# Output matmuls of a gated linear attention: four 32-column tiles in place of two 64-column tiles

## The chip, the cores and the metric

The kernel runs on one core of one Trainium2 chip. The metric is the device time of that core in microseconds (us). Eleven runs of the kernel before in one session took 195.06 to 195.69 us, 0.3% apart. Each timed execution also has a span (first to last instruction of the program, about 2 us shorter than the time) and a mean granted clock of TensorE. A run that is over 1.5% above the fastest of the same kernel counts as slow and is left out of every ratio here. A median here is over all runs, slow ones too.

Names in the profile: PE is TensorE's matmul, PEld its weight load, DVE is VectorE, ACT is ScalarE, POOL is GpSimd, SP is SyncE, which issues most of the transfers ("SPq" is its queue). L303 is line 303 of that kernel's source.

## The reference

A gated linear attention (4 batches, 8 heads, 768 steps, head size 48) feeds a matmul, a gate h·cos(h), and a second matmul (3072 tokens, 384 → 2048 → 384).

```python
for t in range(S):
    state = alpha[:, :, t, :, None] * state + einsum('bhd,bhe->bhde', k[:, :, t], v[:, :, t])
    y[:, :, t] = einsum('bhd,bhde->bhe', q[:, :, t], state)
# x: y as [3072 tokens, 384]
h = x @ w_in
out = (h * cos(h)) @ w_out
```

## The kernel before

The sequence is cut into 24 chunks of 128 steps (6 per batch). The kernel is a list of units in a hand-made order, one string for all engines; the letter names the unit, the number the chunk (or pair of chunks).

```python
ORDER = """
k1 a0 a3 a1 k0 v1 q0 a2 q2 i0 x12 c0 v3 d0 k2 M0 i1 x7 c1 k3 K0 d1 q1 K1 q3 P1 O0 x13 T0 v0 l1 t0
... (cut)
m9 E6 S9 D10 P11 Q4 u9 b9 D11 V24 z4 R12 V25 u10 v13 H18 K12 v14 b10 H16 D12 h18 H19 q15 g18 h16 o5
... (cut)
"""
```

Units that matter here: `a k q v` load one chunk of alpha, keys, queries and values; `K R` scale keys and queries on POOL; `D` transposes them by DMA; `A` and `m` make and mask the scores; `S u b` compute the state; **`Y` (one chunk) and `Q` (two chunks) are the output matmuls**, `z` copies their result out of PSUM; `H h g` are the first matmuls, the activation and the gate; `V e o` are the second matmuls, their copy and the store; `x` is a fixed number of warm-up matmuls.

The output of a chunk, transposed, is 384 rows (8 heads x 48) by 128 steps, kept as three groups of 128 PSUM partitions. Each row gets two contributions: U, from the state of earlier chunks (one matmul for a pair of heads, absent in the first chunk of a batch), and V, from the scores inside the chunk (one matmul per head). The kernel before splits the 128 partitions into two column tiles of 64:

```python
    def outputs(j, t):
        ...                                   # vs: values, padded; U: state; qT, A: moving operands
        mms = []
        for n in range(2 * 3):                # six tiles of 64 rows
            g, tt = n // 3, n % 3
            a = []
            if j % NC != 0:
                for p, c0 in (((0, 0),), ((0, 64), (1, 96)), ((1, 160),))[tt]:
                    c0 += 2 * C * g
                    a.append((U[:, c0 : c0 + 64], qT[...]))
            for r in range(2):
                ...
                a.append((vs[:, c0 : c0 + 64], A[...]))
            mms.append(a)
        streams = [...]                       # tiles 0, 2, 4 to partitions 0-63; 1, 3, 5 to 64-127
        for i in range(max(map(len, streams))):
            for half, stream in enumerate(streams):
                if i < len(stream):
                    kt, start, stop, lhsT, rhs = stream[i]
                    nc.tensor.matmul(t[64 * half : 64 * half + 64, kt * C : (kt + 1) * C],
                                     lhsT, rhs, start=start, stop=stop, skip_group_check=True)
```

The boundaries of 64 rows cut across heads of 48, so a tile needs 2 V and 1 or 2 U matmuls: 12 V + 8 U = 20 in a chunk, 10 in each stream. A weight load goes with every matmul (448 of each in the trace).

## Time and profile before

| | before |
|---|---|
| median time | 195.58 us (195.28 to 195.73, 4 runs) |
| PE busy, share of the span | 95% |
| output matmuls | 448, in 13 bursts (Y0, Y1, Q1 to Q11) |
| one burst of 40 (Q), first to last start | 1.088 us |

The page of the kernel before, its busy times (us, share of the span, instructions) and its chain of waits (the chain of work that ended last, by engine and by line):

```profile
PE 182.5 (95%) x1990; PEld 131.8 (68%) x1994; DVE 117.7 (61%) x138; ACT 120.1 (62%) x133; POOL 81.6 (42%) x128
...
PE 66%; DMA 13%; SPq 6%; ACT 4%; issue 4%; DVE 3%; POOL 2%; ACTq 0%; DVEq 0%
PE one L362 31%; PE two L341 21%; DMA w<-in_moe_w_out_dram 10%; PE two L303 6%; SPq L158 5%; PE two L243 3%; DVE g_sb L352 3%; DMA v_sb<-in_v_dram 2%; ACT c_sb L347 2%; PE two L191 2%; SPq L161 2%; ACT L347 1%; PE one L257 1%; POOL w L167 1%; PE two L193 1%
```

A busy PE alone would not prove a bound, since ends of matmuls are modelled; the chain shows that from 43 us on the time mostly follows PE. Four stretches of it (59 to 64, 85 to 88, 111 to 117 and 127 to 131 us) pass mainly through ACT and DVE, most of it the gate, and PE waits at their ends for 0.13, 1.0, 0.83 and 0.05 us. L303, the output matmuls, holds 6% of the chain. The same chain in order of time (start us, length us, what), its output bursts Q4 and Q7 alone:

```profile
80.61 1.24 PE two L303 x40
...
123.96 1.24 PE two L303 x40
```

The windows of the second half (window, its length, busy us and instructions per engine, granted clock, DMA share, GB/s):

```profile
124.00:164.00 40.00, 39.95 (x455) 29.68 (x455) 27.76 (x28) 33.92 (x35) 19.80 (x30) 1.00 0.87 162
```

PE has 0.05 us to spare in 40; the other engines have 6 us or more. By these numbers a microsecond less of PE work here should be a microsecond less of time, as long as the others keep up; that is an estimate.

The groups of L303 (out<-in, tile, moving shape, count | busy us, mean ns | idle before):

```profile
L303 PE MATMUL two<-A_sb,vpb 128*64 128x128 bf16 x264 | 13.2, 220 | 0.1
L303 PE MATMUL two<-qkT,ub 128*64 128x128 bf16 x152 | 11.8, 222 | 0.7 <-POOL ub L262 0.7
...
L303 PEld LDWEIGHTS <-vpb 128*64 128x64 bf16 x288 | 12.8, 110 | 0.5 <-issue 0.3
```

The 220 ns is the length of one matmul's record; the starts in one tile lie only 56 ns apart, so the cost is read from the starts. Of burst Q7, ns from its first start, read from the trace:

```
before:  0 4 | 80 83 | 137 140 | 192 195 | 247 251 | ...   pairs, 56 ns apart
```

Two tiles start mostly 3 to 4 ns apart and both take their next matmul 56 ns later: a row of two costs 56 ns. The first step alone is 80 ns.

### The profile page before, as it was taken

The numbers are of one execution on the slowest core, as the hardware profiler recorded it, in microseconds if no ns is written. First come the engines' busy times: TensorE is split into PE (matmuls) and PEld (weight loads), VectorE is DVE, ScalarE is ACT, GpSimd is POOL, SyncE is SP. The second block draws the span as 40 slices with busy tenths as digits, with TensorE's granted clock in tenths as the row PEclk, the third lists the DMA queues.
The fourth block names the chain that finished last, engine by engine and source line by source line (L and its number), as shares of the span: only waits on it lengthen the run. The fifth ranks groups of instructions, "written<-read, shape, count | busy, mean of one in ns | idle before, by whom it ended". The sixth has DMA issues, their size and how long they took to land.

```text
span 192.9 us, 4781 instructions
## 1 busy us (share of the span) xinstructions
PE 182.5 (95%) x1990; PEld 131.8 (68%) x1994; DVE 117.7 (61%) x138; ACT 120.1 (62%) x133; POOL 81.6 (42%) x128
## 2 busy tenths in 40 slices
PE   7997889989999999997999998999999999999993
PEld 2444468957688687685777685786786786876861
DVE  5025784844847928829828438748758578596450
ACT  2540344744768668947739567789999982361632
POOL 3317950055294655571190656271239761030000
PEclk9999999999999999999999999999999999999999
DMA  6999999999989999999989999999998762200112
GB/s 127 188 187 188 146 190 188 184 196 194 190 192 176 205 233 207 188 168 196 268 162 192 175 214 218 175 227 205 149 217 158 135 152 34 85 0 3 41 41 82
DMA packets 123092, 31.23 MB, mean 162 GB/s; under 512 B 117184, under 2 KB 122304, under 8 KB 123072
## 3 DMA queue, kind: packets, MB, share of 16 engines
q1 hardware_dynamic: 120192, 27.80, 85.0%
q0 software_dynamic: 2880, 3.15, 10.1%
q8 instruction: 15, 0.25, 0.5%
q14 instruction: 5, 0.04, 0.1%
HBM read 25.17 MB, written 4.72 MB: 155 GB/s over the span
## 4 chain that ended last, share of the span: by engine, by line
PE 66%; DMA 13%; SPq 6%; ACT 4%; issue 4%; DVE 3%; POOL 2%; ACTq 0%; DVEq 0%
PE one L362 31%; PE two L341 21%; DMA w<-in_moe_w_out_dram 10%; PE two L303 6%; SPq L158 5%; PE two L243 3%; DVE g_sb L352 3%; DMA v_sb<-in_v_dram 2%; ACT c_sb L347 2%; PE two L191 2%; SPq L161 2%; ACT L347 1%; PE one L257 1%; POOL w L167 1%; PE two L193 1%
## 5 line engine op out<-in xcount | busy, mean ns | idle before, releaser
L352 DVE TENSOR_TENSOR g_sb<-two,c_sb 128x1024 bf16<-128x1024 f32 x48 | 58.0, 1221 | 27.7 <-ACT c_sb L347 27.2
L362 PE MATMUL one<-w,g_sb 128*128 128x384 bf16 x384 | 69.5, 327 | 1.4 <-DVE g_sb L352 0.8
L341 PE MATMUL two<-xT,w 128*128 128x256 bf16 (+1 forms) x624 | 68.4, 264 | 1.0 <-DVE g_sb L352 1.0
L347 ACT ACTIVATE c_sb<-two,halfpi 128x1024 bf16<-128x1024 f32 x48 | 52.6, 1113 | 19.5 <-PE two L341 19.0
L341 PEld LDWEIGHTS <-w 128*128 128x128 bf16 x624 | 56.7, 98 | 9.7 <-issue 1.1
L362 PEld LDWEIGHTS <-g_sb 128*128 128x128 bf16 x384 | 35.3, 98 | 24.0 <-DVE g_sb L352 1.7
L206 POOL TENSOR_TENSOR kqb<-k_sb,icp 128x384 bf16<-128x384 f32 x24 | 23.9, 997 | 20.5 <-DMA k_sb<-in_k_dram 12.6
L262 POOL TENSOR_TENSOR ub<-sc,Em 128x384 bf16<-128x384 f32 x20 | 16.6, 829 | 33.1 <-DVE sc L272 31.8
L248 DVE TENSOR_TENSOR A_sb<-two,mask_f 128x1024 bf16<-128x1024 f32 x24 | 28.5, 1217 | 2.6 <-PE two L243 2.6
L212 POOL TENSOR_TENSOR kqb<-q_sb,cp 128x384 bf16<-128x384 f32 x22 | 21.9, 998 | 9.4 <-DMA q_sb<-in_q_dram 5.7
L366 ACT ACTIVATE o_sb<-one 128x384 f32<-128x384 f32 x24 | 11.7, 492 | 15.5 <-PE one L362 15.5
L347 ACT ACT_TABLE_LOAD x11 | 14.1, 1283 | 9.9 <-PE two L341 6.2
L216 POOL CAST vpb<-v_sb 128x384 bf16<-128x384 f32 x24 | 12.0, 504 | 17.2 <-DMA v_sb<-in_v_dram 9.3
L375 PE MATMUL one<-warm 128*128 128x512 bf16 x62 | 17.1, 418 | 2.2 <-DVE warm L102 1.2
L185 ACT ACTIVATE lnab<-a_sb 128x768 bf16<-128x768 f32 (+1 forms) x13 | 10.3, 794 | 12.5 <-DMA a_sb<-in_alpha_dram 12.4
L201 ACT ACTIVATE icp<-two 128x768 f32<-128x768 f32 (+1 forms) x13 | 9.9, 761 | 11.8 <-PE two L193 9.0
L272 DVE TENSOR_TENSOR sc<-one,ub 128x384 f32<-128x384 f32 x20 | 11.0, 552 | 8.2 <-PE one L257 7.9
L321 DVE CAST xT<-two 128x768 bf16<-128x768 f32 x11 | 10.5, 958 | 8.4 <-PE two L303 8.4
L179 ACT ACT_TABLE_LOAD x11 | 14.1, 1283 | 0.9 <-PEq L404 0.7
L303 PE MATMUL two<-A_sb,vpb 128*64 128x128 bf16 x264 | 13.2, 220 | 0.1
L303 PEld LDWEIGHTS <-vpb 128*64 128x64 bf16 x288 | 12.8, 110 | 0.5 <-issue 0.3
L375 PEld LDWEIGHTS <-warm 128*128 128x128 bf16 x66 | 6.4, 104 | 9.6 <-issue 3.6
(42 smaller groups left out, 114.1 us busy)
## 6 DMA issues: line engine op xcount, KB each, us to landing
k_sb<-in_k_dram SPq DMA_DIRECT2D x24, 192.0 KB, 4.6
a_sb<-in_alpha_dram SPq DMA_DIRECT2D x24, 192.0 KB, 4.3
v_sb<-in_v_dram SPq DMA_DIRECT2D x24, 192.0 KB, 4.4
q_sb<-in_q_dram SPq DMA_DIRECT2D x24, 192.0 KB, 4.2
out_dram<-o_sb SPq DMA_DIRECT2D x24, 192.0 KB, 3.7
w<-in_moe_w_in_dram POOLq DMA_DIRECT2D x2, 768.0 KB, 10.0
w<-in_moe_w_out_dram POOLq DMA_DIRECT2D x2, 768.0 KB, 17.7
qkT<-kqb SPq DMA_TRANSPOSE x16, 3.8
```

The costliest lines, as they stand in the source:

```text
L179: nc.scalar.preload_act_table_set("natural_log_exp_and_others")
L206: nc.gpsimd.tensor_tensor(out=kqb[j % 4][:, 0, :, 0:D], in0=k_t[j % 6], in1=icp_t[j // 2 % 3][:, j % 2].rearrange("s (h d) -> s h d", h=H) ...
L212: eng.tensor_tensor(out=kqb[j % 4][:, 1, :, 0:D], in0=q_t[j % 6], in1=cp.rearrange("s (h d) -> s h d", h=H), op=ALU.mult)
L216: nc.gpsimd.tensor_copy(out=vpb[j % 4][:, :, 0:D], in_=v_t[j % 6])
L248: nc.vector.tensor_tensor(out=A_t[j % 4].rearrange("s (h t) -> s h t", h=H), in0=two[("A", j)].rearrange("s (h t) -> s h t", h=H), in1=mas ...
L262: eng.tensor_tensor(out=ub[j % 3][:, :, 0:96].rearrange("r p (a e) -> r p a e", a=2), in0=src.rearrange("r p (a e) -> r p a e", a=2), in1= ...
L303: nc.tensor.matmul(t[64 * half : 64 * half + 64, kt * C : (kt + 1) * C], lhsT, rhs, start=start, stop=stop, skip_group_check=True)
L341: nc.tensor.matmul(t[:, m * n : (m + 1) * n], w1[:, kk, f * C : (f + 1) * C], x_t[g % 3][:, kk, bs].rearrange("r b t -> r (b t)"), start=( ...
L347: nc.scalar.activation(out=c_s.take((name, i)), in_=two[(name, i)], func=AF.Sin, bias=halfpi, scale=1.0)
L352: nc.vector.tensor_tensor(out=g_t[g % 3][:, fs, bs], in0=shaped(two[(name, i)], name), in1=shaped(c_s[(name, i)], name), op=ALU.mult)
L362: nc.tensor.matmul(one[("o", j)][:, 0:DM], g_t[j // 2 % 3][:, f, j % 2], w2[:, f], start=(f == 0), stop=(f == NF - 1))
L375: nc.tensor.matmul((one.free or two.free)[0][:, 0:512], warm[:, 0:C], warm, start=True, stop=True)
```

## The change

Cut the 128 partitions into four column tiles of 32 rows. With 32-row groups a pair of heads (96 rows) is exactly three groups: rows 0-31 of the first head, its rows 32-47 with rows 0-15 of the second, rows 16-47 of the second. Each group needs one U and 1, 2 or 1 V: 12 U + 16 V = 28 matmuls a chunk, more than before, but in four streams of 7 in place of two of 10. Over the kernel 448 matmuls become 624.

```diff
-        for n in range(2 * 3):
-            g, tt = n // 3, n % 3
-            ... (cut)
+        def group(g):
+            p, r = g // 3, g % 3
+            mms = []
             if j % NC != 0:
+                mms.append((U[:, p * C + 32 * r : p * C + 32 * r + 32],
+                            qT[:, (NP + p) * C : (NP + p + 1) * C]))
+            for h, off in (((0, 0),), ((0, 32), (1, -16)), ((1, 16),))[r]:
+                h += 2 * p
+                mms.append((vs[:, h * VS + off : h * VS + off + 32],
+                            A[:, ACOL[h] * C : (ACOL[h] + 1) * C]))
+            return [(g // 4, i == 0, i == len(mms) - 1) + m for i, m in enumerate(mms)]
+
+        streams = [sum((group(g) for g in range(c, 12, 4)), []) for c in range(4)]
         for i in range(max(map(len, streams))):
-            for half, stream in enumerate(streams):
+            for c, stream in enumerate(streams):
                 if i < len(stream):
                     kt, start, stop, lhsT, rhs = stream[i]
-                    nc.tensor.matmul(t[64 * half : 64 * half + 64, kt * C : (kt + 1) * C],
-                                     lhsT, rhs, start=start, stop=stop, skip_group_check=True)
+                    nc.tensor.matmul(t[32 * c : 32 * c + 32, kt * C : (kt + 1) * C],
+                                     lhsT, rhs, start=start, stop=stop, skip_group_check=True,
+                                     tile_position=(0, 32 * c))
```

The rest of the diff adds a unit that scales keys on DVE; the order string does not use it and is unchanged.

More of the change, by code (lines that the diff above doesn't have):

```diff
@@ L203, in exps, with scale_k @@
         two.give(("c", j))
-    def scale_k(j):
-        nc.gpsimd.tensor_tensor(out=kqb[j % 4][:, 0, :, 0:D], in0=k_t[j % 6],
+    def scale_k(eng, j):
+        eng.tensor_tensor(out=kqb[j % 4][:, 0, :, 0:D], in0=k_t[j % 6],
                                 in1=icp_t[j // 2 % 3][:, j % 2].rearrange("s (h d) -> s h d", h=H),
@@ L279, in outputs @@
         U = ub[(j - 1) % 3].rearrange("r p e -> r (p e)")
-        mms = []
-        for n in range(2 * 3):
-            g, tt = n // 3, n % 3
-            a = []
+        def group(g):
+            p, r = g // 3, g % 3
+            mms = []
             if j % NC != 0:
-                for p, c0 in (((0, 0),), ((0, 64), (1, 96)), ((1, 160),))[tt]:
-                    c0 += 2 * C * g
-                    a.append((U[:, c0 : c0 + 64],
-                              qT[:, (NP + 2 * g + p) * C : (NP + 2 * g + p + 1) * C]))
-            for r in range(2):
-                h = 4 * g + (2 * tt + r + 1) // 2
-                c0 = 4 * VS * g + 64 * (2 * tt + r)
-                a.append((vs[:, c0 : c0 + 64], A[:, ACOL[h] * C : (ACOL[h] + 1) * C]))
-            mms.append(a)
-        streams = [
-            [(n // 2, i == 0, i == len(mms[n]) - 1) + m
-             for n in range(half, 6, 2) for i, m in enumerate(mms[n])]
-            for half in range(2)
-        ]
+                mms.append((U[:, p * C + 32 * r : p * C + 32 * r + 32],
[6 more added lines that the diff above has]
+        streams = [sum((group(g) for g in range(c, 12, 4)), []) for c in range(4)]
         for i in range(max(map(len, streams))):
-            for half, stream in enumerate(streams):
+            for c, stream in enumerate(streams):
                 if i < len(stream):
                     kt, start, stop, lhsT, rhs = stream[i]
-                    nc.tensor.matmul(t[64 * half : 64 * half + 64, kt * C : (kt + 1) * C],
-                                     lhsT, rhs, start=start, stop=stop, skip_group_check=True)
+                    nc.tensor.matmul(t[32 * c : 32 * c + 32, kt * C : (kt + 1) * C],
+                                     lhsT, rhs, start=start, stop=stop, skip_group_check=True,
+                                     tile_position=(0, 32 * c))
     def outputs_one(j):
@@ L379 @@
         "l": lambda g: ln(2 * g, 2), "C": lambda g: cums(2 * g, 2), "E": lambda g: exps(2 * g, 2),
-        "K": scale_k, "R": lambda j: scale_q(nc.gpsimd, j), "O": lambda j: scale_q(nc.vector, j),
+        "K": lambda j: scale_k(nc.gpsimd, j), "B": lambda j: scale_k(nc.vector, j), "R": lambda j: scale_q(nc.gpsimd, j), "O": lambda j: scale_q(nc.vector, j),
         "P": cast_v, "M": decay,
```

## The prediction

> **What bounds the kernel now.** TensorE, after a DMA-bound start. The page gives PE 95% busy; the chain of waits that ended last is 66% PE, 13% DMA. In order of time that chain runs through loads until 42.8 us, then almost only through PE, up to 190 us. From 124 to 164 us, by windows, PE is busy in all but 0.05 us, ACT in 34 us, DVE in 28 us.
>
> **What the output matmuls cost.** The timeline of PE has 13 bursts of line 303: Y0, Y1, Q1 before 28 us, then ten (Q2 to Q11), all on the chain. A burst of 40 matmuls has 1.088 us between its first and last start, one of 32 has 0.865 us (chain: 1.24 and 1.01 us with entry and exit). The starts come in pairs, 3 to 4 ns apart, and the pairs 56 ns apart. So both tiles run side by side, and a stream costs 56 ns per 128-column matmul: 20 rows x 56 = 1.12 us.
>
> **What the change does.** For a chunk with a carried state 20 matmuls in two streams of 10 become 28 in four streams of 7; for the first chunk of a batch 12 (6 and 6) become 16 (4 each). In all 448 become 624, each with its weight load: 352 instructions more. The schedule string is unchanged; the new vector-engine variant of the key scaling is not called. Per Q burst: 20 rows become 14, or 16 become 11. At 56 ns a row, plus about 7 ns for two more starts in the last row, I estimate 1.088 -> 0.76 us and 0.865 -> 0.59 us. Saved: 7 x 0.33 + 3 x 0.27 = 3.1 us on the chain; Y0, Y1 and Q1 lie where the chain waits for DMA and gain nothing.
>
> **Does a row of four stay at 56 ns?** [...] The weight load of 64 columns precedes its matmul by about 53 ns[...]. The risk is supply: 28 pairs in 0.4 us is 14 ns a pair, and nothing here has run faster than 28 ns a pair over a burst; one-column matmuls of line 193 come every 25 ns. If 25 ns were a floor, 56 pairs would take 1.4 us a loss of about 3 us in all. [...]I give this one in five.
>
> **How much arrives.** Some K and V loads land 0.1 us before use, and PE waits about 1 us for the gate multiply near 88 and 117 us. Estimate: 85%, 2.65 us.
>
> Predicted: 192.8 us, 191.4 to 195.4. Faster by over 2%: 0.07; within 2%: 0.90; slower by over 2%: 0.03.
>
> **What will show it.** Line 303: 624 matmuls, starts in fours 3 to 4 ns apart, rows 56 ns; Q bursts 0.9 and 0.75 us in the chain; weight loads under 110 ns.
>
> **What would make it wrong.** Rows of four longer than 56 ns (a supply floor, or weight loads of four tiles not overlapping): line 303 then keeps or exceeds 1.24 us. Or rows as predicted, but new idle time of PE eats the gain.

That a row of four would stay at 56 ns is my estimate; the trace showed rows of two. 7 x 0.33 + 3 x 0.27 = 3.1 us, 85% of it 2.65 us, taken from the 195.45 us that was the median of three runs at the time, is 192.8 us.

## The result

The changed kernel took 193.18 us in the median (192.79 to 193.83, 4 runs) against 195.58 us (195.28 to 195.73, 4 runs). The ratio is 0.9882, with a 95% interval of 0.9852 to 0.9913: 2.4 us less, a little over 1%. A ratio here is the mean time of one kernel's fast runs over that of the other's fast runs of the same rounds, so it is not quite the ratio of the medians.

In the changed kernel L303 has become L298, L341 is L337, L352 is L348 and L362 is L358. Its page:

```profile
PE 180.2 (94%) x2170; PEld 128.3 (67%) x2170; DVE 117.7 (62%) x138; ACT 119.9 (63%) x133; POOL 81.5 (43%) x128
...
PE 72%; DVE 7%; ACT 7%; SPq 6%; issue 4%; DMA 2%; POOL 0%; DVEq 0%; ACTq 0%
PE one L358 32%; PE two L337 24%; PE two L298 4%; SPq L158 4%; DVE g_sb L348 3%; PE two L243 3%; PE one L371 3%; ACT c_sb L343 3%; DMA q_sb<-in_q_dram 2%; ACT L343 2%; PE two L191 2%; SPq L161 2%; PE one L257 1%; DVE qkT L232 1%; PE one L227 1%
```

Output matmuls went from 6% of the chain to 4%, with 176 more matmuls. (The shares of DMA, 13% and 2%, differ because the chain takes another path through the loads before 43 us; that is not read as an effect of the change.) The same two bursts in the chain:

```profile
80.64 1.06 PE two L298 x56
...
123.30 0.90 PE two L298 x56
```

Q7 takes 0.90 in place of 1.24 us, as do most; Q4 is the exception: 1.06. The groups:

```profile
L298 PE MATMUL two<-A_sb,vpb 128*32 128x128 bf16 x352 | 9.8, 220 | 0.2 <-DVE A_sb L248 0.2
L298 PE MATMUL two<-qkT,ub 128*32 128x128 bf16 x228 | 9.3, 221 | 0.9 <-POOL ub L262 0.9
...
L298 PEld LDWEIGHTS <-vpb 128*32 128x32 bf16 x384 | 8.8, 96 | 1.1 <-issue 0.7
```

In the middle of Q4 the V matmuls of its second chunk now come before DVE has masked their scores: DVE (L248) ends at 81.13 us, their row starts at 81.19, 0.21 us after the row before in place of 0.056, a wait of 0.16 us. The slower burst before had just hidden it: DVE ended at 81.10 us there, and the first of these V matmuls came at 81.18. (The 0.2 us in the last column is a wait in Q1, at 27.57 us.) The starts of Q7:

```
changed: 0 4 7 10 | 67 69 74 77 | 123 125 129 133 | ...    fours, 56 ns apart
```

All four tiles start within 10 ns and the row still takes 56 ns. The first step fell from 80 to 67 ns. Between the loads of the first and second row in one tile lie 15 ns now (in Q2) and 29 ns before (in Q4), from the traces. Over the ten bursts Q2 to Q11, the time from first to last start sums to 10.21 us before and 7.13 us after, 3.09 us less.

So 3.09 us were saved where the chain runs, and 2.4 us (2.1 us in the repeat below) arrived. To see where the rest went, compare when PE reaches fixed points of its program: the start of given weight loads, us, and in the other columns the difference to before, from the traces (the two right-hand kernels are experiments below).

```
point of PE's program        before  changed  e4_after  e11_k19_again
last warm-up but a few        28.54    +1.30     -0.12          +1.28
second matmuls, 33rd          47.10    +0.61     +0.04          +0.58
first matmuls, 193rd          69.22    +0.03     -0.53          +0.01
first matmuls, 337th         111.98    -0.66     -1.23          -0.69
first matmuls, 385th         126.28    -1.00     -1.57          -0.64
first matmuls, 433rd         139.79    -1.35     -1.83          -0.61
second matmuls, 257th        144.37    -1.35     -1.18          -0.61
second matmuls, 289th        157.61    -1.46     -1.03          -0.73
end                          192.95    -2.16     -1.73          -1.13
```

Two things stand out. The profiled run of the change was 1.30 us late at 28 us and 0.61 us late at 47 us; after that it gained 2.77 us. In it the clock was granted at 0.72 between 20 and 26 us (1.00 before), while warm-up matmuls ran; its mean was 0.991, and two of eleven runs of the kernel before in the next session have the same mean, so this is a matter of the run, not of the change. And in the repeat, without that delay, PE gained steadily to 140 us and then gave back 0.65 us at one point.

A caution on the table: the traced run of the kernel before took 195.0 us, less than the median of its timed runs (195.58), so the row "end" shows less than the medians do. What happens after 47 us can be compared all the same. In the profiles of two experiments below that keep the slow bursts there, the same points lie at +0.57 to +0.58 us (`e1_early`) and +0.35 to +0.36 us (`e9_before_k19k20`) from 47 us to the end: with the slow bursts nothing varies there by more than 0.01 us. With the fast bursts, PE keeps 2.77 of the 3.09 us in this profile, 1.77 in `e4_after` and 1.83 in `e2_late`.

### The profile page after: what moved, and what is told of

It reads as the page before. It is cut to its first block, busy times and chain, and to the rows that moved or that the text cites. A ratio compares the mean times of both kernels' runs of the same rounds, so it can differ in the third digit from the quotient of the medians.

```text
span 190.8 us, 5137 instructions
## 1 busy us (share of the span) xinstructions
PE 180.2 (94%) x2170; PEld 128.3 (67%) x2170; DVE 117.7 (62%) x138; ACT 119.9 (63%) x133; POOL 81.5 (43%) x128
## 4 chain that ended last, share of the span: by engine, by line
PE 72%; DVE 7%; ACT 7%; SPq 6%; issue 4%; DMA 2%; POOL 0%; DVEq 0%; ACTq 0%
PE one L358 32%; PE two L337 24%; PE two L298 4%; SPq L158 4%; DVE g_sb L348 3%; PE two L243 3%; PE one L371 3%; ACT c_sb L343 3%; DMA q_sb<-in_q_dram 2%; ACT L343 2%; PE two L191 2%; SPq L161 2%; PE one L257 1%; DVE qkT L232 1%; PE one L227 1%
## 5 line engine op out<-in xcount | busy, mean ns | idle before, releaser
L348 DVE TENSOR_TENSOR g_sb<-two,c_sb 128x1024 bf16<-128x1024 f32 x48 | 58.0, 1221 | 27.7 <-ACT c_sb L343 27.1
L358 PE MATMUL one<-w,g_sb 128*128 128x384 bf16 x384 | 69.5, 327 | 1.1 <-DVE g_sb L348 1.0
L337 PE MATMUL two<-xT,w 128*128 128x256 bf16 (+1 forms) x624 | 68.4, 265 | 1.0 <-DVE g_sb L348 1.0
L337 PEld LDWEIGHTS <-w 128*128 128x128 bf16 x624 | 56.7, 98 | 9.7 <-issue 1.1
L358 PEld LDWEIGHTS <-g_sb 128*128 128x128 bf16 x384 | 35.4, 98 | 23.6 <-DVE g_sb L348 2.0
L248 DVE TENSOR_TENSOR A_sb<-two,mask_f 128x1024 bf16<-128x1024 f32 x24 | 28.5, 1217 | 2.6 <-PE two L243 2.6
L371 PE MATMUL one<-warm 128*128 128x512 bf16 x66 | 18.5, 430 | 1.9 <-DVE warm L102 1.2
L362 ACT ACTIVATE o_sb<-one 128x384 f32<-128x384 f32 x24 | 11.5, 493 | 13.6 <-PE one L358 13.5
L272 DVE TENSOR_TENSOR sc<-one,ub 128x384 f32<-128x384 f32 x20 | 11.0, 552 | 8.2 <-PE one L257 7.8
L298 PE MATMUL two<-qkT,ub 128*32 128x128 bf16 x228 | 9.3, 221 | 0.9 <-POOL ub L262 0.9
L298 PE MATMUL two<-A_sb,vpb 128*32 128x128 bf16 x352 | 9.8, 220 | 0.2 <-DVE A_sb L248 0.2
```

Source lines behind the costliest of these rows:

```text
L248: nc.vector.tensor_tensor(out=A_t[j % 4].rearrange("s (h t) -> s h t", h=H), in0=two[("A", j)].rearrange("s (h t) -> s h t", h=H), in1=mas ...
L298: nc.tensor.matmul(t[32 * c : 32 * c + 32, kt * C : (kt + 1) * C], lhsT, rhs, start=start, stop=stop, skip_group_check=True, tile_position ...
L337: nc.tensor.matmul(t[:, m * n : (m + 1) * n], w1[:, kk, f * C : (f + 1) * C], x_t[g % 3][:, kk, bs].rearrange("r b t -> r (b t)"), start=( ...
L348: nc.vector.tensor_tensor(out=g_t[g % 3][:, fs, bs], in0=shaped(two[(name, i)], name), in1=shaped(c_s[(name, i)], name), op=ALU.mult)
L358: nc.tensor.matmul(one[("o", j)][:, 0:DM], g_t[j // 2 % 3][:, f, j % 2], w2[:, f], start=(f == 0), stop=(f == NF - 1))
L371: nc.tensor.matmul((one.free or two.free)[0][:, 0:512], warm[:, 0:C], warm, start=True, stop=True)
```

## The experiments

Twelve runs were made, of ten kernels beside the two given. Unless a line says otherwise the results were correct and each was timed in five rounds against the kernel before on the same chip.

### Which bursts count

`e1_early` uses the four-tile form only in the chunks of Y0, Y1 and Q1, `e2_late` only in those of Q2 to Q11; `e4_after` is the changed kernel again.

```diff
+    def outputs(j, t):
+        (outputs_narrow if j < 4 else outputs_wide)(j, t)     # e1_early; e2_late: the other way round
```

> Four 32-column tiles only in the first three bursts (Y0, Y1, Q1, before 30 us); the ten later bursts stay as before. Theory (those bursts lie where the chain of waits is bound by loads and fixed warm-up work, so their saving is lost): ratio to before 0.998 to 1.002. Rival (every shortened burst counts, 0.5 to 0.6 us in all): ratio 0.997 or lower, about 194.9 us.

> Four 32-column tiles only in the ten bursts Q2 to Q11. Theory: the whole gain of the change, ratio to before 0.984 to 0.990, equal to the full change within 0.3%. Rival (the early part, where the changed kernel's profile was about 1.3 us late at 25 us, costs or gives a share): the two differ by more than 0.3%.

> The changed kernel again, unaltered, as a yardstick on the same chip: ratio 0.985 to 0.991, that is 192.8 to 193.8 us.

Measured: `e1_early` 195.36 us, ratio 0.9998 (0.9985 to 1.0011). `e2_late` 193.07 us, 0.9887 (0.9862 to 0.9911; one slow run of 196.31 us left out). `e4_after` 193.33 us, 0.9896 (0.9883 to 0.9909). The early bursts are worth nothing and the ten late ones are the whole change; both rivals fall. The early delay is not tied to the change: `e1_early`'s profile has it, that of the unaltered change, `e4_after`, does not.

### Is it the number of tiles, or the narrow weights?

`e3_pairs` has the same 28 matmuls on the same four tiles, with two streams issued to their end before the other two.

```diff
-        for i in range(max(map(len, streams))):
-            for c, stream in enumerate(streams):
+        for cs in ((0, 1), (2, 3)):
+            for i in range(max(map(len, streams))):
+                for c in cs:
```

> The same 28 matmuls a chunk on the same four 32-column tiles, but issued as two pairs of streams one after the other, so that two tiles run at a time. Theory (a row costs 56 ns whatever the width of its tiles, and the gain is only the fewer rows): 28 rows for Q bursts in place of 20 before and 14 changed; first to last start about 1.53 us (before 1.088, changed 0.747); time about 195.5 + 4 = 199.5 us, ratio 1.015 to 1.025. Rival (narrower weight loads are what pays, and concurrency of four adds little): bursts at or under 1.09 us and a ratio of at most 1.0.

Measured: 194.78 us, ratio 0.9968 (0.9940 to 0.9996), a burst 0.927 us. Both numbers miss my theory's range and lie in the rival's. But the rival's reason does not hold either: had narrow weights paid, matmuls of one tile would follow each other faster, and they still lie 56 ns apart. What failed is an assumption that both had made, that matmuls start in program order. The timeline of PE in burst Q2 (start us, length us, ..., count):

```profile
53.95 0.23 PE L299 MATMUL two<-qkT,ub 128*32 128x128 bf16 x2
54.01 0.22 PE L299 MATMUL two<-A_sb,vpb 128*32 128x128 bf16 x2
54.07 0.22 PE L299 MATMUL two<-qkT,ub 128*32 128x128 bf16 x1
54.07 0.27 PE L299 MATMUL two<-A_sb,vpb 128*32 128x128 bf16 x2
54.13 0.24 PE L299 MATMUL two<-qkT,ub 128*32 128x128 bf16 x3
54.18 0.24 PE L299 MATMUL two<-A_sb,vpb 128*32 128x128 bf16 x4
```

Call a matmul on `ub` U and one on `vpb` V. The first two streams are, in program order, UU VV UV VU **VV** UU VV; then the other two begin, UU VV... The record has UU VV UV VU, then **UU**, 6 ns after the fourth row, and only then VV. The extra U can only be those of the other two streams: they started at 54.13 us, ahead of six older matmuls (12 instructions with their loads), the first of which come at 54.18 us. So two streams overlap the next two. If so, whole streams in sequence must overlap as well:

```diff
-        for cs in ((0, 1), (2, 3)):
+        for cs in ((0,), (1,), (2,), (3,)):
```

> The changed kernel's 28 matmuls a chunk, with the four streams in program order one whole stream after the other, 7 matmuls each. Theory from the run with pairs of streams (matmuls of an idle tile start ahead of older ones that wait for a busy tile, within some 12 instructions): about two tiles at a time, 28 x 56 / 2 = 0.78 us a chunk, 1.5 to 1.7 us from first to last start of a burst of 56, ratio 1.02 to 1.03. Rival (matmuls start strictly in program order): 56 x 56 ns = 3.1 us a burst, ratio 1.10 or more. Rival (the order in the program does not matter at all): 0.75 us, ratio 0.99.

Measured (three rounds): 199.66 us, ratio 1.0237 (1.0210 to 1.0264), a burst 1.632 us. That is the theory's range, and strict program order (3.1 us) is refuted. The starts in Q2 (U and V as above; the order in the program is U V U V V U V for stream 0, then U V V U V U V for stream 1):

```
0U 66V 122U 177V | 183U 233V 250V 289U 306V 345V | 362U 367U ...
```

Stream 1 begins at 183, 6 ns after the fourth matmul of stream 0, with three of that stream still to come. In chunks without U, whose streams have four matmuls, all four streams begin at once, 13 to 14 ns apart. In both patterns a stream begins when three matmuls of the stream before it are still to come; in `e3_pairs`, too, it was three in each of the two tiles. By what rule PE chooses is not shown. Order within the program mattered less than strict program order would have it (1.632 us in place of 3.1), and the interleaving that the change uses is the best of the three orders: 0.747, 0.927 and 1.632 us.

What then do these runs show? A tile took one 128-column matmul every 56 ns, at 64 columns (before) and at 32 (changed, `e3_pairs`, `e5_serial`), and tiles ran side by side, their starts 2 to 5 ns apart. With the streams interleaved, a burst cost about 56 ns times the matmuls of the fullest tile: 20 before (1.12 us by that count, 1.088 from first to last start), 14 changed (0.78 and 0.747).

### How close together can pairs start?

The prediction's main doubt was that PE might not be fed 28 pairs of weight load and matmul in 0.4 us. `e6_n64` cuts every output matmul into two of 64 moving columns, `e6_n32` into four of 32 (three rounds each).

```diff
+            for m in range(2):                                # e6_n32: 4
                 for c, stream in enumerate(streams):
+                        s = slice(m * C // 2, (m + 1) * C // 2)
-                    nc.tensor.matmul(t[32 * c : 32 * c + 32, kt * C : (kt + 1) * C],
-                                     lhsT, rhs, ...)
+                        nc.tensor.matmul(t[32 * c : 32 * c + 32, kt * C : (kt + 1) * C][:, s],
+                                         lhsT, rhs[:, s], ...)
```

> The changed kernel with every output matmul cut into two of 64 moving columns, each with its own weight load: 112 pairs of weight load and matmul in a burst in place of 56, the same arithmetic. Theory (a row is bound by streaming its columns; the supply of instructions is no limit): rows of about 29 ns [...], 7 ns a pair; burst about 0.80 us from first to last start, as the changed kernel's 0.75; ratio 0.988 to 0.992. Rival (supply binds at the 14 ns a pair that the change needs, which is all that has been seen over a whole burst): 1.55 us a burst, ratio 1.025 to 1.035. Rival (25 ns a pair, as the one-column matmuls came): 2.8 us, ratio about 1.09.

> The same with four matmuls of 32 moving columns: 224 pairs in a burst. [...] Theory: here a limit other than streaming shows, since one-column matmuls in one tile came every 25 ns; rows of about 25 ns, 6 ns a pair, 1.4 us a burst, ratio 1.01 to 1.03. If supply holds it at 7 to 14 ns a pair: 1.6 to 3.1 us, ratio 1.03 to 1.12.

The first text's 29 ns and 0.80 us stand as estimates: half of the measured 56 ns is 28 ns, and 28 such rows are 0.78 us. "Supply" and "streaming" are the theories' names for causes; the runs show starts alone.

Both gave wrong results (relative error 0.20 and 0.22). Why is not shown: no run here tests it. The instructions and their operands are the intended ones, so I use the starts, not the results.

Measured: `e6_n64` 199.11 us, ratio 1.0159 (1.0109 to 1.0210), its profiled run slow; a burst 0.918 us. `e6_n32` 239.70 us, ratio 1.2158 (1.2098 to 1.2217; two slow runs left out); bursts of 1.55 to 5.43 us. In both the first 32 to 38 pairs come in rows of four, 29 ns apart (64 columns) and 25 ns apart (32 columns). Then the rows dissolve and one pair comes every 8.3 to 8.4 ns, on average. The starts of `e6_n64` in Q2 (ns):

```
0 3 7 10 | 39 42 46 49 | 68 71 75 78 | ... | 243 246 250 255 | 273 275 283 292 302 308 317 325 333 341 350 ...
```

The later rate is the same at 64 and at 32 moving columns, so the number of columns does not set it; what does is not shown. The change has a pair every 14 ns (four in 56), and its bursts of 56 pairs keep near that to the end (0.75 us, Q4 apart).

My theory for `e6_n64` (0.80 us a burst, ratio 0.988 to 0.992) missed on both counts, and so did its rivals. The bursts do not explain its time: the ten late ones sum to 8.57 us, less than the 10.21 us before. In its profile PE is 5.0 us late at 47 us, after a stop of 2.84 us at 28 us and 6.8 us at half the clock from 30 us on; from there to the 289th second matmul (161 us) it gains 1.35 us on the kernel before. That profile is of a slow run, so how its fast runs lose their time is not shown.

The time of `e6_n32` has a second cause. Its waits (who waited for what: us in total, times, longest):

```profile
PEld L300 <- issue: 29.0, 12, 5.6
PE two L300 <- issue: 27.4, 10, 5.5
```

"issue" is idle time for which the profile shows no cause. In Q2, for one, PE stands from 65.8 to 69.2 us:

```profile
65.77 0.20 PE L300 MATMUL two<-A_sb,vpb 128*32 128x32 bf16 x3
69.16 0.19 PE L300 MATMUL two<-qkT,ub 128*32 128x32 bf16 x1 [3.19 <-issue]
```

A packet of 16,384 bytes on the instruction queue starts at 66.5 us and takes 1.3 us. There are more of these packets the more instructions the profile counts: 15 for 4781 before, 17 for 5137 in the changed kernel, 22 for 6381 in `e6_n64`, 31 for 8877 in `e6_n32`. The page's line of that queue (packets, MB, share) before, changed and in `e6_n32`:

```profile
q8 instruction: 15, 0.25, 0.5%
```

```profile
q8 instruction: 17, 0.28, 0.6%
```

```profile
q8 instruction: 31, 0.51, 0.9%
```

In each of the nine stops of PE over 1 us in `e6_n32`, and in the one of `e6_n64`, such a packet starts during the stop or at most 1 us before it. That is where the stops lie; what causes them is not shown, and no run tests it alone. In the changed kernel no burst after 43 us has such a stop (PE is not idle in one for 0.05 us); two more packets cost it nothing that shows. My theory for `e6_n32` (1.4 us a burst, ratio 1.01 to 1.03) was wrong: right about the rows of 25 ns, blind to the 8.3 ns and to the stops. The alternative in the same text, 7 to 14 ns a pair, had the rate right.

### Where the rest of the gain goes

In `e4_after` PE waits once for POOL's scaling of a key chunk; so it does in `e2_late`'s profile (0.62 us at 140 us), but not in the first profile of the change. PE and POOL of `e4_after` (start us, length, operation, in brackets idle time and what ended it):

```profile
139.42 0.33 PE L257 MATMUL one<-vpb,kqb 128*128 128x96 bf16 x4
140.50 0.34 PE L257 MATMUL one<-vpb,kqb 128*128 128x96 bf16 x4 [0.75 <-POOL kqb L206]
```

```profile
139.45 0.99 POOL L206 TENSOR_TENSOR kqb<-k_sb,icp 128x384 bf16<-128x384 f32 x1 [6.03 <-DMA k_sb<-in_k_dram]
```

Before, POOL waited for the same load too, but 2.6 us earlier, and PE did not stop:

```profile
136.88 1.00 POOL L206 TENSOR_TENSOR kqb<-k_sb,icp 128x384 bf16<-128x384 f32 x1 [5.69 <-DMA k_sb<-in_k_dram]
```

PE had got 1.8 us ahead, but the load was 2.6 us later. The program gives the queue that issues it one long list, and that queue did not speed up with PE: it issued this load at 132.50 us before and at 135.09 us in `e4_after`. The issue, before and in `e4_after`, with the transpose before it:

```profile
129.11 1.86 SPq L236 DMA_TRANSPOSE qkT<-kqb  x1
...
132.50 0.81 SPq L158 DMA_DIRECT2D k_sb<-in_k_dram  x1
```

```profile
131.46 2.49 SPq L236 DMA_TRANSPOSE qkT<-kqb  x1
...
135.09 0.68 SPq L158 DMA_DIRECT2D k_sb<-in_k_dram  x1
```

Its issue times vary from run to run: 136.2 us in `e1_early`, which keeps the slow bursts here, 134.2 us in the first profile of the change. A DMA transpose holds the queue for 1.2 to 3.4 us in `e4_after`. Three experiments move loads: `e7_k19` exchanges this load with an alpha load that was early; `e8_k19k20` also exchanges the next key load with an early query load; `e9_before_k19k20` does both to the kernel before.

```diff
-... v18 A15 A14 a23 m15 ...        ... h30 k19 P18 ...
+... v18 A15 A14 k19 m15 ...        ... h30 a23 P18 ...
-... H29 q23 P19 ...                ... C10 k20 Q8 ...        (e8 and e9 only)
+... H29 k20 P19 ...                ... C10 q23 Q8 ...
```

> The changed kernel with one pair of loads exchanged in the load queue: the K load of chunk 19, issued at 135.1 us and landed at 139.4 us just before its use in the repeated run of the changed kernel, takes the earlier place of an alpha load that is needed only near 148 us. Theory (the wait for this load gives back about 0.65 us of the saving at 140 us): PE no longer waits there, the offset of PE against before stays near -1.8 us from 136 to 150 us, and the time falls by 0.4 to 0.8 us against the unaltered change, ratio to before 0.985 to 0.988. Rival (the DMA engines as a whole bound this stretch, whatever their order, so another load is late in its place): no fall, ratio 0.989 to 0.991.

> As the one before, and the K load of chunk 20 exchanged with a Q load that lay 13 us ahead of its use. Theory: the second give-back of about 0.3 us near 155 us goes too; ratio 0.983 to 0.987, about 192.4 us, which keeps 2.7 to 3.0 us of the 3.1 us that the bursts save. Rival (order of loads does not matter): 0.989 to 0.991.

> Control: the same two exchanges of loads in the kernel before. Theory (there PE never waited for these loads, since its slower bursts hid them; they bind only once PE is faster): ratio 0.998 to 1.002. Rival (the exchange is a gain of its own, not tied to the change): ratio 0.997 or lower.

Measured: `e7_k19` 192.42 us, ratio 0.9853 (0.9835 to 0.9872), its profiled run slow and left out. `e8_k19k20` 192.76 us, 0.9888 (0.9858 to 0.9919). `e9_before_k19k20` 195.09 us, 0.9989 (0.9969 to 1.0009). The control is as expected: the exchange is worth nothing without the change. The first supports the theory; the second, although it contains the first, came out between the two ranges, and its interval covers both. So I ran the first again:

> The version with the K load of chunk 19 earlier once more, since its profile fell in the slow state and the version with both loads exchanged, which contains it, came out nearer to the unaltered change (0.9888) than it did (0.9853). Theory (the wait for this load gave back about 0.65 us): ratio 0.984 to 0.988 again, and a profile of the fast state in which PE does not wait for a K scaling near 140 us. Rival (0.9853 was luck and the exchange is worth nothing): 0.989 to 0.991.

Measured: 193.08 us, ratio 0.9880 (0.9862 to 0.9897), at the very edge of the theory's range. The wait at 140 us is gone from its profile, and POOL scales that chunk at 134.81 us:

```profile
134.81 1.00 POOL L206 TENSOR_TENSOR kqb<-k_sb,icp 128x384 bf16<-128x384 f32 x1
```

But 0.75 us of this run's lead goes elsewhere, between 112 and 140 us, where the right-hand column of the table of points stands still (-0.69 to -0.61) while two bursts save 0.7 us. The chain of this run passes there through the queue and the load of the key chunk before (start us, length us, what):

```profile
122.02 2.49 DMA k_sb<-in_k_dram
...
126.82 1.00 POOL kqb L206
127.81 1.91 POOL kqb L212 x2
...
129.88 0.80 POOL ub L262
130.70 0.57 DVE sc L272
...
131.31 0.81 PE one L358 x4
```

What is shown: the wait at 140 us cost 0.65 us in one run, and moving that load removes that wait. What is not: that the exchange makes the kernel faster. Of three timings with it, on other chips than the repeat, one is below the unaltered change and two are level with it (0.9853, 0.9880, 0.9888 against 0.9882 and 0.9896); the interval of the lowest is clear of the repeat's, not of the first measurement's. In `e11_k19_again` the rival holds in part: with one load taken forward, another was late in its place. In `e8_k19k20`'s profile (192.48 us) it was not: PE keeps 2.51 of the 3.09 us after 47 us there.

One more attempt moved the burst Q4 behind a group of second matmuls (`V24`), so that the mask it waits for is done, on top of `e7_k19`:

```diff
-m9 E6 S9 D10 P11 Q4 u9 b9 D11 V24 z4
+m9 E6 S9 D10 P11 u9 b9 D11 V24 Q4 z4
```

> The version with the K load of chunk 19 earlier, and the burst Q4 moved behind one group of the second matmuls, so that the mask multiply that it waited for in its middle (about 0.16 us, near 81 us) is done. Theory: the burst takes 0.75 us from first to last start in place of 0.91; time 0.1 to 0.2 us under the version with the load alone, about 192.3 us, ratio 0.983 to 0.987: within noise of it. Rival (the later burst delays the first matmuls of its pair of chunks): ratio above 0.987.

Measured: 193.72 us, ratio 0.9916 (0.9897 to 0.9934). Q4 did take 0.746 us, but the group moved ahead of it waits 1.0 us:

```profile
81.30 0.81 PE L358 MATMUL one<-w,g_sb 128*128 128x384 bf16 x4 [1.01 <-DVE sc L272]
```

V24 opens a new output in a PSUM tile that DVE's state addition (L272) reads before, and PE now waits 1.01 us for it; Q4 had been the work that covered that wait. A miss: I had looked at one wait and not at what the burst itself was hiding.

No version tried is shown to be faster than the change as given; it and its variants with earlier loads beat the kernel before by about 1%.

## Why the prediction was right

The prediction was 192.8 us (191.4 to 195.4) and "within 2%" at 0.90; measured were 193.18 us and a ratio of 0.9882. Point by point:

- **PE bounds the kernel after the start.** Right. `e2_late` (0.9887) carries the whole change, `e1_early` (0.9998) none.
- **A row of four takes what a row of two took, 56 ns.** Right: 2 to 5 ns between tiles, 56 ns between rows. In `e3_pairs` and `e5_serial` too the matmuls of one tile lie 56 ns apart, with weights of 32 columns as with 64 before.
- **Bursts of 0.76 and 0.59 us, 3.1 us in all.** Measured 0.747 and 0.579 us, and 3.09 us in all with Q4's wait counted in. The supply risk, one in five, did not come: the change starts a pair every 14 ns, and `e6_n64` and `e6_n32` went on at one every 8.3 to 8.4 ns after their first rows.
- **Weight loads under 110 ns.** Right, 96 ns on average in the group above, 110 before. The 53 ns from load to matmul did not change with the width: the second row's load precedes its matmul by 53 ns at 64 columns and at 32. What the 53 ns consist of is not shown; what shrank is the first step, by 13 ns.
- **85% arrives, 2.65 us.** This is the term that was mis-sized: 2.4 us in the first measurement and 2.1 us in the repeat (medians 195.41 and 193.33), 78% and 67% of 3.09. The interval of the first measurement (1.7 to 2.9 us) still holds 2.65; that of the repeat (1.8 to 2.3 us) does not. The causes named were two. The gate waits near 88 and 117 us were there before and after, unchanged (1.0 and 0.83 us in `e4_after`), so they cost nothing extra. But a new gate wait came, near 156 us: 0.28 us in `e4_after` and `e2_late`, 0.17 us in the first profile, none before. Of the late K and V loads one K load shows: 0.65 us at 140 us in `e4_after`, and, when it was moved, another K load in `e11_k19_again`; PE is not seen to wait for a V load. How much each costs changes with the run, and the sum of about 0.7 to 1.0 us is not settled further.

## What to carry to other kernels

Count matmuls per tile, not matmuls: here 56 in four interleaved streams of 14 took 0.747 us where 40 in two of 20 took 1.088, and the same 56 one stream after the other took 1.632. Test how far that goes: past some 32 pairs the smaller matmuls of `e6_n64` and `e6_n32` came no faster than one pair in 8.3 ns. When the bounding engine gets faster, look at once at the queue that issues its loads: here PE was 1.8 us ahead, one key load was issued 2.6 us later than before, and loads that had landed 0.1 us before use (0.07 to 0.14 us in the trace before) can be the next wait, 0.65 us in `e4_after`. Before moving a burst to spare it a wait, look for the wait that the burst itself covers (1.01 us for V24 in `e10_k19_q4`).
